# Gate folded into the attention values and the FFN, down and output projections in one bank, and an early third integer buffer, in a fused attention and gated-FFN kernel

## Chip, cores, metric

One core of one Trainium2 chip. The metric is the device time of the whole program in microseconds (us), as the median of several executions.

The engines by their short names: PE (TensorE, matrix products), ACT (ScalarE, activation functions), DVE (VectorE, elementwise), POOL (GpSimd), SP (the engine that here only issues DMAs).

## The reference

```python
g = sigmoid((x * gate_w).sum(-1, keepdims=True))          # x: 1 x 2048 x 512, bf16
q, k, v = split_heads(x @ wqkv)                           # 32 heads of width 16
p = softmax(q @ k.T * 16**-0.5);  a = (p @ v) @ wo
b = ((x @ w_gate) * (x @ w_up)) @ w_down                  # 512 -> 1376 -> 512
out = g * a + (1 - g) * b
```

Inputs are bf16. The exponentials dominate: 32 heads x 2048 x 2048.

## The kernel before

A small planner inside the kernel's Python code simulates the engines with fixed durations and fixes one static order of instructions for each engine. On the chip every engine works through its list in order and waits on semaphores. Whatever stands first in a list blocks all that is behind it.

The exponentials are done in *units* of 128 keys x 512 queries for one head; four units (four heads) of one key range are a *key tile*. There are 2048 units. ACT computes most with its Exp, two or three per instruction. DVE computes the others with integer arithmetic: four clamps from PSUM into an int16 buffer, and four shifted tables from that buffer, whose weighted values PE adds up. So a DVE tile takes four value passes of PE where an ACT tile takes one.

```python
D_START = 45.0                    # no DVE tile earlier on the planner's clock
D_SLOT = 0.3                      # how late DVE may be before a span takes a DVE unit as its third
FFN_FROM, FFN_TO = 60.0, 490.0    # FFN products due evenly over these key tiles
...
nb = (dst["buf"] + 1) % (3 if "k" in last_v else 2)     # third int16 buffer (wk) only after the last K product
...
# up: psX -> usb (copy);  gate: psX * usb -> hT;  down: psX * omg[:, t] -> bsb;  output: psX * gval[:, t] + bsb -> ost
...
def norm(m, last):                # after the last value pass of head group m
    for j in range(4):            # SP: numerators into place, then the denominators
        a = P.dma("sp", onum[r0 : r0 + 16, :] <- oraw[r0 : r0 + 16, s, :], dur=0.3)
    a = P.dma("sp", den[...] <- oraw[dr : 96 + dr + 1 : 32, s, :])
...                               # cut and abridged
def finish(...):                  # DVE: rec = 1 / den;  SP: rec -> DRAM -> rb, broadcast;  POOL: OT = onum * rb
...
fl.append((20, mk_gate(20)))      # gate unit due at key tile 20; Q of the second head block is due at 18
```

The softmax here doesn't subtract the row's maximum and nothing guards it: scores larger than these inputs give would overflow.

## Time and profile before

Three runs: 760.57 us median (760.49 to 761.5).

| | value | view |
|---|---|---|
| ACT busy | 735.3 us, 97% | first page |
| PE / DVE busy | 706.6 us (93%) / 677.7 us (89%) | first page |
| clamp copies, i.e. units on DVE | 440 of 2048 | groups |
| ACT in 168 to 740 us | busy 571.0 of 572 us | windows |

From the first page: the span, the busy time of each engine (us, share, instructions), and the chain of work that ended last.

```profile
span 759.2 us, 20945 instructions
...
PE 706.6 (93%) x8946; PEld 213.3 (28%) x8946; DVE 677.7 (89%) x1116; ACT 735.3 (97%) x672; POOL 65.2 (9%) x73
...
ACT 31%; DVE 30%; PE 30%; issue 6%; SPq 1%; DMA 1%; DVEq 0%; ACTq 0%
...
```

All three compute engines are close to full, and the chain passes through each of them for about 30%. From the groups by form (line, engine, operation, output<-input, shapes, count | busy us, mean ns of one | idle before it):

```profile
...
L1477 ACT ACTIVATE PT<-psS 128x1536 bf16<-128x1536 f32 x275 | 399.2, 1534 | 3.1 <-PE psS L889 2.8
L1477 ACT ACTIVATE PT<-psS 128x1024 bf16<-128x1024 f32 x386 | 386.9, 1111 | 5.6 <-PE psS L889 4.4 <-PE psX L985 0.7 <-PE psO L1120 0.2
...
L1042 DVE TENSOR_SCALAR SC<-SC 128x2048 int16<-128x2048 int16 x316 | 213.1, 692 | 2.2
L1013 DVE TENSOR_SCALAR SC<-psS 128x512 int16<-128x512 f32 x256 | 172.1, 682 | 15.1 <-PE psS L889 13.0 <-PE psX L985 1.6
...
L632 DVE CAST usb<-psX 128x512 bf16<-128x512 f32 x40 | 27.2, 680 | 0.8 <-PE psX L370 0.8
...
L683 DVE TENSOR_SCALAR bsb<-psX,omg 128x512 bf16<-128x512 f32 x16 | 11.6, 725 | 0.0
...
L708 DVE SCALAR_TENSOR_TENSOR ost<-psX,gval,bsb 128x512 bf16<-128x512 f32 x12 | 8.9, 743 | 2.5 <-PE psX L370 2.5
...
```

The table (L1042) and the clamp (L1013) take 0.69 and 0.68 us each on DVE; the up eviction (L632) 0.680, the scaled down eviction (L683) 0.725 and the combine (L708) 0.743. L1477 is the exponential in its three-unit and two-unit form. An ACT instruction overlaps the next by about 0.1 us. Measured from start to start where nothing waits, a two-unit exponential takes 0.904 us and a three-unit one 1.331 us. With these, the exponentials of this kernel are 720 us of pure ACT work. What the span has beyond that, from the first exponential on, is called *excess*: 29 us here, most of it before 140 us and in the last 10 us.

The windows early and in the main part (length, then busy time and instruction count of each engine, granted PE clock, DMA share and rate):

```profile
...
45.00:168.00 123.00, 112.11 (x1286) 31.95 (x1282) 102.63 (x167) 116.41 (x104) 5.44 (x4) 0.89 0.06 15
168.00:740.00 572.00, 538.10 (x6833) 159.95 (x6829) 548.30 (x901) 571.02 (x525) 17.08 (x13) 1.00 0.08 20
...
```

```profile
...
L509 SPq DMA_DIRECT2D QX<-Qst x8: 581/589/644, 44.0 to 48.5; - x8
...
DMA to landing us min/median/max: 1.8/1.8/3.0
```

DVE has 20 us to spare before 168 us and 24 us after.

### The profile page before, as it was taken

The numbers are of one execution on the slowest core, as the hardware profiler recorded it, in microseconds if no ns is written. First come the engines' busy times: TensorE is split into PE (matmuls) and PEld (weight loads), VectorE is DVE, ScalarE is ACT, GpSimd is POOL, SyncE is SP. The second block draws the span as 40 slices with busy tenths as digits, with TensorE's granted clock in tenths as the row PEclk, the third lists the DMA queues.
The fourth block names the chain that finished last, engine by engine and source line by source line (L and its number), as shares of the span: only waits on it lengthen the run. The fifth ranks groups of instructions, "written<-read, shape, count | busy, mean of one in ns | idle before, by whom it ended". The sixth has DMA issues, their size and how long they took to land.

```text
span 759.2 us, 20945 instructions
## 1 busy us (share of the span) xinstructions
PE 706.6 (93%) x8946; PEld 213.3 (28%) x8946; DVE 677.7 (89%) x1116; ACT 735.3 (97%) x672; POOL 65.2 (9%) x73
## 2 busy tenths in 40 slices
PE   9998898999899999998999999998999989899997
PEld 3322222222222322222222222222222222222243
DVE  3449987989999999999989989999999989999994
ACT  6989999999999999999999999999999999999995
POOL 8940000000000000000000000000000000000000
PEclk9978898999999999999999999999999999999999
DMA  8900000000010010101001010000001100010000
GB/s 173 284 16 9 16 15 25 16 9 24 9 30 9 23 38 11 29 9 28 12 10 31 29 30 10 24 15 9 24 10 28 40 19 16 7 29 8 24 23 31
DMA packets 32881, 22.81 MB, mean 30 GB/s; under 512 B 20468, under 2 KB 27572, under 8 KB 32788
## 3 DMA queue, kind: packets, MB, share of 16 engines
q1 hardware_dynamic: 31476, 20.42, 10.3%
q8 instruction: 71, 1.16, 0.7%
q0 software_dynamic: 256, 0.79, 0.4%
q10 hardware_dynamic: 1056, 0.26, 0.2%
q14 instruction: 22, 0.18, 0.1%
HBM read 11.24 MB, written 2.35 MB: 18 GB/s over the span
## 4 chain that ended last, share of the span: by engine, by line
ACT 31%; DVE 30%; PE 30%; issue 6%; SPq 1%; DMA 1%; DVEq 0%; ACTq 0%
ACT PT L1477 31%; DVE SC L1042 10%; PE psS L889 9%; DVE SC L1013 9%; PE psX L370 9%; PE psO L1120 8%; DVE wk L1013 4%; PE psS L370 1%; DVE hT L645 1%; DVE usb L632 1%; SPq L1180 1%; DVE wk L1042 1%; DMA den<-oraw 1%; DVE oraw L1173 1%; PE psO L1130 1%
## 5 line engine op out<-in xcount | busy, mean ns | idle before, releaser
L1477 ACT ACTIVATE PT<-psS 128x1024 bf16<-128x1024 f32 (+1 forms) x662 | 727.5, 1286 | 8.7 <-PE psS L889 7.2
L889 PE MATMUL psS<-QX,KT 32*128 32x512 bf16 x1966 | 265.0, 390 | 32.8 <-ACT PT L1477 21.3
L1042 DVE TENSOR_SCALAR SC<-SC 128x2048 int16<-128x2048 int16 x316 | 213.1, 692 | 2.2
L1013 DVE TENSOR_SCALAR SC<-psS 128x512 int16<-128x512 f32 x256 | 172.1, 682 | 15.1 <-PE psS L889 13.0
L1120 PE MATMUL psO<-PT,VV 128*32 128x512 bf16 x1546 | 150.1, 391 | 1.2 <-DVE oraw L1173 0.6
L889 PEld LDWEIGHTS psS<-QX,KT 32*128 32x128 bf16 x1966 | 68.6, 91 | 290.4 <-ACT PT L1477 113.9
L1120 PE MATMUL psO<-SC,VD 128*32 128x512 bf16 x1140 | 106.7, 389 | 4.1 <-DVE SC L1042 3.6
L1233 POOL TENSOR_TENSOR OT<-onum,rb 128x512 bf16<-128x512 f32 x16 | 21.3, 1332 | 674.0 <-DMA rb<-rscr 674.0
L1013 DVE TENSOR_SCALAR wk<-psS 128x512 int16<-128x512 f32 x102 | 68.5, 680 | 1.0 <-PE psS L889 0.7
L1042 DVE TENSOR_SCALAR SC<-wk 128x2048 int16<-128x2048 int16 x93 | 62.1, 688 | 0.1
L1120 PEld LDWEIGHTS psO<-PT,VV 128*32 128x32 bf16 x1546 | 38.6, 95 | 59.0 <-issue 48.2
L370 PE MATMUL psX<-xT,wu 128*32 128x512 bf16 x688 | 53.1, 394 | 1.0 <-DVE SC L1013 0.4
L370 PE MATMUL psX<-wd,hT 128*32 128x512 bf16 (+1 forms) x704 | 52.8, 382 | 0.1
L370 PE MATMUL psX<-xT,wg 128*32 128x512 bf16 x688 | 51.1, 383 | 0.6 <-DVE usb L632 0.2
L1120 PE MATMUL psO<-SC,VV 128*32 128x512 bf16 x428 | 43.3, 395 | 2.6 <-DVE oraw L1173 1.4
L1013 DVE TENSOR_SCALAR SC<-psX 128x512 int16<-128x512 f32 x60 | 40.7, 679 | 2.6 <-PE psX L985 2.6
L1120 PEld LDWEIGHTS psO<-SC,VD 128*32 128x32 bf16 x1140 | 28.1, 95 | 46.7 <-DVE SC L1042 27.2
L645 DVE TENSOR_TENSOR hT<-psX,usb 128x512 bf16<-128x512 f32 (+1 forms) x44 | 29.9, 680 | 3.6 <-PE psX L370 3.5
L985 PE MATMUL psX<-QX,KT 32*128 32x512 bf16 x82 | 32.2, 392 | 0.6 <-DVE hT L645 0.2
L632 DVE CAST usb<-psX 128x512 bf16<-128x512 f32 (+1 forms) x44 | 29.9, 680 | 0.8 <-PE psX L370 0.8
L1042 DVE TENSOR_SCALAR wk<-wk 128x2048 int16<-128x2048 int16 x31 | 21.8, 704 | 0.7
L1173 DVE COPY oraw<-psO 128x512 f32<-128x512 f32 x31 | 21.1, 681 | 0.5 <-PE psO L1120 0.5
(115 smaller groups left out, 363.9 us busy)
## 6 DMA issues: line engine op xcount, KB each, us to landing
rb<-rscr SPq DMA_DIRECT2D x16, 256.0 KB
onum<-oraw SPq DMA_DIRECT2D x124, 32.0 KB, 2.0
QX<-Qst SPq DMA_DIRECT2D x120, 16.0 KB, 1.8
out_dram<-ost SPq DMA_DIRECT2D x12, 128.0 KB, 1.8
wu<-in_B_w_up_dram SPq DMA_DIRECT2D x1, 1376.0 KB, 7.0
wg<-in_B_w_gate_dram SPq DMA_DIRECT2D x1, 1376.0 KB, 9.8
wd<-in_B_w_down_dram SPq DMA_DIRECT2D x1, 1280.0 KB, 12.7
SC<-in_A_x_dram SPq DMA_DIRECT2D x4, 128.0 KB, 3.2
```

The source lines that it names most:

```text
L370: r = pe.matmul(dst_[j : j + 32, :], lhs[:, j : j + 32], rhs, start=s0, stop=s1, tile_position=(0, j), skip_group_check=True,)
L632: "dve", lambda v: v.tensor_copy(usb[0:w, n % 2, :], un.bank[0:w, :]), deps, **EV
L645: lambda v: v.tensor_tensor(hT[0:w, f, :], un.bank[0:w, :], usb[0:w, n % 2, :], ALU.mult),
L889: q = pe.matmul(bank_ap(sl, k_), KT[32 * j : 32 * j + 32, b, kt * 128 : (kt + 1) * 128], QX[32 * j : 32 * j + 32, p, b, :], start=True, st ...
L985: lambda pe: pe.matmul(bank, KT[32 * j : 32 * j + 32, b, kt * 128 : (kt + 1) * 128], QX[32 * j : 32 * j + 32, p, b, :], start=True, stop=True,
L1013: lambda v: v.tensor_scalar(i2b(nb)[:, j, :], bank, _LO, _HI, ALU.max, ALU.min),
L1042: lambda v: v.tensor_scalar(dstt, src, 0.5, _BASE + _OFF[k], ALU.mult, ALU.add),
L1120: r = pe.matmul(psO[r_, :], vcol(m, kt, k_, j), pj, start=first, stop=last, tile_position=(0, 32 * j), skip_group_check=True)
L1130: r = pe.matmul(psO[r_, 256 * hf : 256 * hf + 256] if w < 2 else psD[r_, 0:256], vcol(m, kt, k_, j, hf) if w < 2 else ones[:, k_, 16 - 16 ...
L1173: o_ev[m] = P.op("dve", lambda v: v.tensor_copy(oraw[:, s, :], psO[:]), deps, **EV)
L1233: lambda g: g.tensor_tensor(OT[:, c % 2, b, :], onum[:], rb[:], ALU.mult),
L1477: lambda a: a.activation(cell_ap(cells[0], n).rearrange("p a b -> p (a b)"), bank_ap(sl, 0, n), ACT.Exp, scale=_LN2 / _OCT,),
```

## The change

Four intents. (1) Multiply the attention's normalisation by g and the up product by 1 - g, so that down and output projections accumulate in one PSUM bank with a single eviction. (2) Let `bsb` serve as a third integer buffer until `wk` is free, and start DVE tiles earlier. (3) Looser rules for giving DVE a unit. (4) A new timetable for the FFN products, Q projections six tiles earlier, the gate at tile 16 instead of 20, and value passes under more pressure. The core of the diff, cut:

```diff
-    D_START = 45.0
+    D_START = 38.0
-    D_SLOT = 0.3
+    D_SLOT = 0.6
-    FFN_FROM, FFN_TO = 60.0, 490.0
+    FFN = [(64, 160, 164, 5), (184, 270, 275, 5), (295, 385, 395, 4), (412, 478, 480, 5)]
+    gsc = nc.dram_tensor("gscr", [2, S], F32, kind="Internal").ap()
...
+                        for i, src_ in enumerate([gval, omg]):
+                            o = P.dma("pool", lambda e, i=i, src_=src_: e.dma_start(
+                                    gsc[i].rearrange("(t p) -> p t", p=128), src_[:], allow_slow_non_contiguous=True),
+                                [ogate["g"]], "dgs", dur=1.0, lat=20.0)
+                        ...   # 8 loads gscr -> gC (g beside the denominators), 1 load gscr -> omgB (1 - g, broadcast; 3 more follow later)
...
-                            "dve", lambda v: v.tensor_copy(usb[0:w, n % 2, :], un.bank[0:w, :]), deps, **EV
+                            lambda v: v.tensor_tensor(usb[0:w, n % 2, :], un.bank[0:w, :], omgB[0:w, :], ALU.mult),
...
+            return Unit(due, chain(FT + NB, mm), deps, drain)          # down and output in one bank, then one copy
...
-            nb = (dst["buf"] + 1) % (3 if "k" in last_v else 2)
+            nb = (dst["buf"] + 1) % 3
+                third[g, kt] = wk_i if "k" in last_v else bsb_i
...
+                r = P.op("dve", lambda v: v.tensor_tensor(rec[:, s, 0:w_], rec[:, s, 0:w_], gC[:, c, 0:w_], ALU.mult), ...)
...
-        fl.append((20, mk_gate(20)))
+        fl.append((16, mk_gate(16)))
-                n0 = 128 * c + 32 * b - 24
+                n0 = 128 * c + 32 * b - 30
...
+            press = sum(q_[1] is None for q_ in p_ring)
-            if pvs and not hold and (not fs or len(tails) or nr >= RP or len(pvs) - nr >= DP):
+            if pvs and not hold and (not fs or len(tails) or press >= RP or len(pvs) - nr >= DP):
```

More of the change, by code (lines that the diff above doesn't have):

```diff
@@ L168, in _build @@
     RU = 24
-    D_START = 45.0
+    D_START = 38.0
+    X_FILL = 45.0
     D_LEFT = 4
@@ L218, in _build @@
         usb = sb("usb", [128, 2, 512], BF16)
-        bsb = sb("bsb", [128, 5, D], BF16)
+        bsb = sb("bsb", [128, 4, D], BF16)
+        omgB = sb("omgB", [128, 512], F32)
+        gC = sb("gC", [128, NCH, 32], F32)
         ost = sb("ost", [128, 2, D], BF16)
@@ L566, in make @@
                             [un.free, o_vd, o_one],
-                            dur=0.75,
+                            dur=1.3,
                         )
@@ L575, in mk_v, with ld_omg @@
             return Unit(due, chain(KD, mm), lambda: [d_wv, ev_x[t]], drain)
-        ogate = {}
+        ogate, o_omg, gate_wait = {}, {}, []
+        def ld_omg(c, deps, eng="sp"):
+            o_omg[c] = P.dma(
+                eng,
+                lambda e: e.dma_start(omgB[:], bass.AP(gsc.tensor, gsc.offset + S + 512 * c, [[0, 128], [1, 512]])),
+                deps,
+                f"domg{c > 0}",
+            )
         def mk_gate(due):
@@ L608, in make @@
                         )
+                        for i, src_ in enumerate([gval, omg]):
+                            o = P.dma(
+                                "pool",
+                                lambda e, i=i, src_=src_: e.dma_start(
+                                    gsc[i].rearrange("(t p) -> p t", p=128), src_[:], allow_slow_non_contiguous=True
+                                ),
+                                [ogate["g"]],
+                                "dgs",
+                                dur=1.0,
+                                lat=20.0,
+                            )
+                        for i in range(8):
+                            p, j = i % 2, i // 2
+                            o1 = P.dma(
+                                "pool",
+                                lambda e, p=p, j=j: e.dma_start(
+                                    gC[32 * j : 32 * j + 32, :, 16 * p : 16 * p + 16],
+                                    bass.AP(gsc.tensor, gsc.offset, [[16, 32], [512, NCH], [1, 16]]),
+                                ),
+                                [o],
+                                "dgc",
+                                dur=1.0,
+                            )
+                        ogate["c"] = o1
+                        for dl in gate_wait:
+                            dl[-1] = o1
+                        ld_omg(0, [o], "pool")
                     dve_push(3, [e1], make)
@@ L627, in drain @@
                 if which == "u":
-                    deps = [last, u_free.get(n - 2)]
+                    deps = [last, u_free.get(n - 2), o_omg[c]]
                     def make():
                         ev_u[n] = un.free = P.op(
-                            "dve", lambda v: v.tensor_copy(usb[0:w, n % 2, :], un.bank[0:w, :]), deps, **EV
-                        )
+                            "dve",
+                            lambda v: v.tensor_tensor(usb[0:w, n % 2, :], un.bank[0:w, :], omgB[0:w, :], ALU.mult),
+                            deps,
+                            **EV,
+                        )
+                        if f == FT - 1 and c < NCH - 1:
+                            ld_omg(c + 1, [un.free])
                     dve_push(2, deps, make)
@@ L654, in deps @@
                 if which == "u":
+                    r.append(o_omg[c])
                     if n >= 2:
@@ L676, in drain @@
                     h_use[c] = last
-                deps = [last, ogate["g"], b_use.get(t - 5)]
+                deps = [last, last_v.get("b")]
                 def make():
-                    ev_b[t] = un.free = P.op(
-                        "dve",
-                        lambda v: v.tensor_scalar(bsb[:, t % 5, :], un.bank, omg[:, t : t + 1], None, ALU.mult),
-                        deps,
-                        dur=0.65,
-                        lat=0.1,
-                    )
+                    ev_b[t] = un.free = P.op("dve", lambda v: v.tensor_copy(bsb[:, tt, :], un.bank), deps, **EV)
                 dve_push(2, deps, make)
@@ L692, in deps @@
                 r = [d_wd] + [ev_h[c, f] for f in range(FT)]
-                if t >= 5:
-                    r.append(b_use[t - 5])
                 return r
@@ L708, in make @@
                     lambda v: v.scalar_tensor_tensor(
-                        dst, bank, gval[:, t : t + 1], bsb[:, t % 5, :], ALU.mult, ALU.add
+                        dst, bank, gval[:, t : t + 1], bsb[:, t % 4, :], ALU.mult, ALU.add
                     ),
@@ L724, in combine, with mk_dw, mm @@
             dve_push(2, deps, make)
-        def mk_wo(c, tt, due):
+        def mk_dw(c, tt, due):
             t = 4 * c + tt
-            def mm(pe, bk, b, s0, s1):
+            def mm(pe, bk, i, s0, s1):
+                if i < FT:
+                    w = FW[i]
+                    return cmm(pe, bk, hT[0:w, i, tt * 128 : (tt + 1) * 128], wd[0:w, i, :], s0, s1)
+                b = i - FT
                 return cmm(pe, bk, OT[:, c % 2, b, tt * 128 : (tt + 1) * 128], wo[:, b, :], s0, s1)
@@ L733, in drain, with make @@
                 if tt == 3:
-                    ot_use[c] = last
-                combine(t, un.bank, last, un)
+                    ot_use[c] = h_use[c] = last
+                deps = [last, o_out.get(t - 2)]
+                def make():
+                    o_comb[t] = un.free = P.op("dve", lambda v: v.tensor_copy(ost[:, t % 2, :], un.bank), deps, **EV)
+                    o_out[t] = P.dma(
+                        "sp",
+                        lambda e: e.dma_start(out2[t * 128 : (t + 1) * 128, :], ost[:, t % 2, :]),
+                        [o_comb[t]],
+                        f"dout{t % 2}",
+                    )
+                dve_push(2, deps, make)
             def deps():
-                r = [d_wo, ev_b[t]] + [o_mult[c, b] for b in range(NB)]
+                r = [d_wd, d_wo] + [ev_h[c, f] for f in range(FT)] + [o_mult[c, b] for b in range(NB)]
                 if t >= 2:
@@ L741, in deps @@
                 return r
-            return Unit(due, chain(NB, mm), deps, drain)
+            return Unit(due, chain(FT + NB, mm), deps, drain)
         def grp(m):
@@ L753, in _build @@
         on_d = {}
-        st = dict(gA=0, actE=None, actJ=0, gD=0, pvg=0, prog=0, i2=0)
+        st = dict(gA=0, actE=None, actJ=[], gD=0, pvg=0, prog=0, i2=0)
         def kq_deps(m, kt):
@@ L758, in kq_deps, with act_units @@
             return [ev_k[b, kt // 4 - (b == kt == 0)], q_dma[b, c, p]]
-        def act_units(n):
+        def act_units(n, but=None):
+            order = lambda js: sorted(js, key=lambda j: (j == but, j))
             r = []
-            g, e, j = st["gA"], st["actE"], st["actJ"]
+            g, e, js = st["gA"], st["actE"], order(st["actJ"])
             lf = {g: list(left[g])}
@@ L770, in act_units @@
                         break
-                    e, j = (g, lf[g].pop(0)), 0
-                r.append((e, j))
-                j += 1
-                if j == 4:
+                    e, js = (g, lf[g].pop(0)), order(range(4))
+                r.append((e, js.pop(0)))
+                if not js:
                     e = None
@@ L779, in take @@
             for e, j in units:
-                if j == 0:
+                if e != st["actE"]:
                     left[e[0]].remove(e[1])
-                st["actE"], st["actJ"] = (e, j + 1) if j < 3 else (None, 0)
+                    st["actE"], st["actJ"] = e, [0, 1, 2, 3]
+                st["actJ"].remove(j)
+                if not st["actJ"]:
+                    st["actE"] = None
                 st["gA"] = e[0]
@@ L827, in cap @@
         def cap(sl, now):
-            if sl and not xs[1]["res"] and now > D_START:
+            if sl and not xs[1]["res"] and now > X_FILL:
                 x_get(now)
@@ L872, in do_s @@
             if len(un) == 3 and spans and not overdue() and backlog(now) < min(need_s() - now, 1.5) + D_SLOT:
-                busy = {j for _, j in un[:2]}
-                j = d_can(now, busy)
-                if j is not None and j not in busy:
-                    dj, un, dh = j, un[:2], Hold()
+                if dst["e"] is not None or d_claim(now):
+                    for j in dst["js"]:
+                        two = act_units(2, j)
+                        if j not in [j_ for _, j_ in two]:
+                            dj, un, dh = j, two, Hold()
+                            break
             n = len(un)
@@ L929, in _build, with i2b @@
         wk_i = wk[:, :, :].bitcast(I16)
-        def i2b(nb):
-            return I2[:, nb, :, :] if nb < 2 else wk_i
+        bsb_i = bsb[:, :, :].bitcast(I16)
+        third = {}
+        def i2b(e):
+            return I2[:, on_d[e], :, :] if on_d[e] < 2 else third[e]
         def d_can(now, js_busy):
@@ L968, in d_claim @@
             on_d[g, kt] = nb
+            if nb == 2:
+                third[g, kt] = wk_i if "k" in last_v else bsb_i
             dst["cnt"] = 0
@@ L1007, in d_unit @@
                 st["prog"] += 1
-            d4 = [o, d_free[nb] or (last_x[0] if nb < 2 else last_v["k"])]
+            d4 = [o, d_free[nb] or (last_x[0] if nb < 2 else None)]
+            if nb == 2 and third[e] is wk_i:
+                d4.append(last_v["k"])
             def make():
@@ L1012, in make @@
                     "dve",
-                    lambda v: v.tensor_scalar(i2b(nb)[:, j, :], bank, _LO, _HI, ALU.max, ALU.min),
+                    lambda v: v.tensor_scalar(i2b(e)[:, j, :], bank, _LO, _HI, ALU.max, ALU.min),
                     d4,
@@ L1037, in make @@
                 def make():
-                    src = i2b(nb)[:, :, :].rearrange("p a b -> p (a b)")
+                    src = i2b(e)[:, :, :].rearrange("p a b -> p (a b)")
                     dstt = LL[:, k, :, :].rearrange("p a b -> p (a b)") if k < 3 else src
@@ L1042, in make @@
                         lambda v: v.tensor_scalar(dstt, src, 0.5, _BASE + _OFF[k], ALU.mult, ALU.add),
-                        pops + ([lf or last_x[0]] if k < 3 else done[:3]),
+                        pops + ([lf or last_x[0]] if k < 3 else []),
                         dur=0.6,
@@ L1084, in lview @@
             nb = on_d[e]
-            return (LL[:, k, j, :] if k < 3 else i2b(nb)[:, j, :]).bitcast(BF16)
+            return (LL[:, k, j, :] if k < 3 else i2b(e)[:, j, :]).bitcast(BF16)
         def vcol(m, kt, k, j, low=None):
@@ L1146, in do_pv @@
                     d_free[nb] = o
+                    if nb == 2 and third[e] is bsb_i:
+                        last_v["b"] = o
                     dst["p1"][nb] = None
@@ L1209, in make @@
                 r = P.op("dve", lambda v: v.reciprocal(rec[:, s, 0:w_], den[:, s, 0:w_]), dd + [norm_ops.get(("scr", blk - 2))], dur=0.25)
+                if c < NCH - 1:
+                    r = P.op(
+                        "dve",
+                        lambda v: v.tensor_tensor(rec[:, s, 0:w_], rec[:, s, 0:w_], gC[:, c, 0:w_], ALU.mult),
+                        [r, ogate["c"]],
+                    )
                 norm_ops["rec", blk] = r
@@ L1238, in make @@
                     assert c < 2 or (c - 2) in ot_use
-            dve_push(1, dd, make)
+            dl = dd + [ogate.get("c", "pending")]
+            if "c" not in ogate:
+                gate_wait.append(dl)
+            dve_push(1, dl, make)
         fl = []
@@ L1254, in _build @@
             for b in range(NB):
-                n0 = 128 * c + 32 * b - 24
+                n0 = 128 * c + 32 * b - 30
                 fl.append((n0, mk_q(b, c, n0)))
-        n_ffn = NCH * (2 * FT + 4)
-        a0, a1 = FFN_FROM, FFN_TO
-        q = 0
-        for c in range(NCH):
+        for c, (a0, a1, ad, dd) in enumerate(FFN):
             for f in range(FT):
-                for w in "ug":
-                    du = a0 + (a1 - a0) * q / n_ffn
+                for i, w in enumerate("ug"):
+                    du = a0 + (a1 - a0) * (2 * f + i) / (2 * FT)
                     fl.append((du, mk_ug(c, f, w, du)))
-                    q += 1
             for tt in range(4):
-                du = a0 + (a1 - a0) * q / n_ffn
-                fl.append((du, mk_d(c, tt, du)))
-                q += 1
-        for c in range(NCH - 1):
-            fl += [(128 * (c + 1) + 8 + 3 * tt, mk_wo(c, tt, 128 * (c + 1) + 8 + 3 * tt)) for tt in range(4)]
+                du = ad + dd * tt
+                fl.append((du, (mk_dw if c < NCH - 1 else mk_d)(c, tt, du)))
         fl.sort(key=lambda x: x[0])
@@ L1389, in step_pe @@
                 f = pick_fill(t + 0.3)
-                if t > D_START and any(isinstance(x["u"], Unit) for x in xs):
+                if t > X_FILL and any(isinstance(x["u"], Unit) for x in xs):
                     f = None
@@ L1417, in step_pe @@
             if pick == "pv":
-                it = next((q_ for q_ in pvs if (q_[1] is not None) == (nr < RP)), pvs[0])
+                it = next((q_ for q_ in pvs if (q_[1] is not None) == (press < RP)), pvs[0])
                 p_ring.remove(it)
```

## The prediction

> **What bounds the kernel now.** 2048 exponential units (128x512) are shared by two engines. ScalarE (ACT) is the limit: busy 735.3 of 759.2 us (first page), and by windows 571.0 of the 572 us between 168 and 740. Its 24 us of idle time lie in the prologue, in 45 to 140 us (about 6.6) and in the tail (9.7). So time moves by (1) units taken from ACT and (2) those early stalls. By groups ACT takes 1.45 us for three units and 1.00 for two: 0.45 us a unit plus 0.10 an instruction. VectorE (DVE) takes 440 units (the clamp copies), 110 key tiles; each tile needs 4 clamps of 0.68 us and 4 tables of 0.69, 5.45 us for four units that cost ACT 1.8. DVE is busy 677.7 us (89%), PE 706.6 (93%); a DVE tile needs four value passes where an ACT tile needs one, about 0.65 us more PE.
>
> **What the change does.**
> - Down and output projections of chunks 0 to 2 share a bank: twelve scaled evictions (0.73 us) vanish, twelve combines (0.74) become copies (0.68): -9.5 us DVE. PE products stay the same in number.
> - The up eviction becomes a product with an fp32 SBUF operand. The Trainium skill, "VectorE: DVE Perf Modes", section "Why PSUM operands drop a tier", caps fp32 with a PSUM operand at 1x; here the cast and the gate product from PSUM both take 0.680 us, so I expect no change.
> - Twelve gate products on denominators: about 0.18 us each (the 128x16 op took 0.174): +2. Net DVE -7 us.
> - The gate's round trip through DRAM: a few DMAs once, near 45 us. The first normalisation runs at 78 us, so at most a few us of DVE waiting.
> - A third integer buffer from the start instead of at 168 us (first clamp into wk), and DVE tiles from 38 instead of 45 us of the order's own clock. DVE is busy 8.2 of 15 us in 45 to 60, 94.5 of 108 in 60 to 168. I expect about 10 us of DVE idle recovered.
> - The looser slot rule (0.3 to 0.6) and free choice of the quarter let some more DVE units into the main part, where DVE is busy 548 of 572 us: perhaps 5 us.
>
> **Sum.** 7 + 10 + 5 = 22 us of DVE time, 4 more tiles, 16 units: ACT falls by 16 x 0.45 = 7.2 us; more two-unit instructions give back up to 1. Early ACT stalls shrink by 1 to 4. PE gains 2.6 us of work, which it can hold. The changed order of value passes I count as zero.
>
> Predicted: 751 us (-1.3%), 8 in 10 between 743 and 757. Faster by over 2%: 0.18; within 2%: 0.79; slower by over 2%: 0.03.
>
> **What will show it.** Clamp copies 452 to 464 instead of 440; ACT busy 726 to 730 us, still about 97%; DVE about 690 us, 92%; PE 709; up eviction still 0.68 us; bsb evictions four instead of sixteen; clamps into bsb before 168 us; DVE busy in 45 to 168 us up by about 10; ACT idle in 45 to 140 us below 6.
>
> **What would make it wrong.** The fp32 operand makes the up eviction slower (at 0.8 us, +5 us DVE). The gate's DMAs land late, and DVE, in order, stands behind the first normalisation while PE and ACT run dry. The longer hold of the spare bank (15 products in place of 11 or 4) or a crowded middle starves PE. The granted PE clock, 0.66 in 45 to 60 us, falls further or recovers entirely. The order may take many more DVE tiles than I allow: ten more would give 742.

## More of the kernel before

The Q loads of the second head block are issued from 44.0 to 48.5 us and land in 2 us.

## The result

779.23 us median (777.76 to 781.05, four runs) against 761.04 us (760.49 to 762.01, four runs): slower, ratio 1.0239 with a 95% interval of 1.0214 to 1.0264. A ratio here is always the mean time of one kernel's fast runs over that of the other's fast runs of the same rounds, so it is not quite the ratio of the medians quoted.

The first page of the changed kernel (777.4 us):

```profile
span 777.4 us, 21121 instructions
...
PE 715.6 (92%) x8982; PEld 212.3 (27%) x8982; DVE 697.9 (90%) x1164; ACT 729.7 (94%) x680; POOL 75.1 (10%) x84
...
DVE 41%; PE 34%; ACT 12%; DMA 4%; SPq 3%; issue 3%; POOL 1%; DVEq 0%; ACTq 0%
...
```

```profile
...
L1551 ACT ACTIVATE PT<-psS 128x1024 bf16<-128x1024 f32 x434 | 423.2, 1074 | 24.4 <-PE psS L950 22.2 <-PE psX L1052 0.9
L1551 ACT ACTIVATE PT<-psS 128x1536 bf16<-128x1536 f32 x235 | 335.4, 1500 | 7.8 <-PE psS L950 4.3 <-remote 3.1
...
L1111 DVE TENSOR_SCALAR SC<-SC 128x2048 int16<-128x2048 int16 x308 | 206.3, 709 | 4.4 <-remote 2.4 <-PE psO L1189 1.7
L1082 DVE TENSOR_SCALAR SC<-psS 128x512 int16<-128x512 f32 x273 | 183.0, 687 | 17.4 <-PE psS L950 16.7 <-PE psS L1052 0.5
...
L674 DVE TENSOR_TENSOR usb<-psX,omgB 128x512 bf16<-128x512 f32 x40 | 27.5, 687 | 0.2 <-PE psX L374 0.2
...
L782 DVE CAST ost<-psX 128x512 bf16<-128x512 f32 x12 | 8.2, 685 | 0.0
...
L728 DVE CAST bsb<-psX 128x512 bf16<-128x512 f32 x4 | 2.7, 684 | 0.9 <-PE psX L374 0.9
...
L1284 DVE TENSOR_TENSOR rec<-rec,gC 128x32 f32<-128x32 f32 x12 | 2.3, 192 | 0.4
...
```

The work has moved as intended. The sixteen bsb evictions are down to four (L728), the twelve combines became copies (L782), and all the clamp groups together are 464, so DVE has 116 tiles instead of 110. ACT is busy 729.7 instead of 735.3 us, and its pure work fell by 9.8 us, from 719.9 to 710.1. And yet the span is 18 us longer: ACT fell from 97% to 94% and from 31% to 12% of the chain. The excess grew from 29 to 57 us. The windows and the Q loads:

```profile
...
45.00:168.00 123.00, 102.42 (x1171) 28.24 (x1175) 106.66 (x178) 105.98 (x99) 14.86 (x16) 0.90 0.20 18
168.00:740.00 572.00, 537.77 (x6615) 153.50 (x6608) 551.38 (x917) 557.71 (x519) 19.12 (x13) 0.98 0.08 21
...
```

```profile
...
L513 SPq DMA_DIRECT2D QX<-Qst x8: 536/589/642, 53.8 to 58.2; - x8
...
DMA to landing us min/median/max: 13.0/13.6/13.8
```

ACT lost 10.4 us between 45 and 168 us (106.0 instead of 116.4) and 13.3 after it (557.7 instead of 571.0). And a Q load now takes 13 us to land where it took 2. The waits of the changed kernel (engine, line, what it waited for: us in total, times, longest):

```profile
...
ACT PT L1551 <- PE psS L950: 26.5, 26, 9.1
POOL gC L638 <- DMA gscr<-omg: 17.7, 1, 17.7
...
DVE rec L1280 <- DMA den<-oraw: 13.1, 11, 3.9
PE psS L950 <- DMA QX<-Qst: 12.3, 1, 12.3
...
ACT PT L1551 <- remote: 3.1, 1, 3.1
...
DVE SC L1111 <- remote: 2.4, 1, 2.4
...
```

The same view of the kernel before has no wait of PE for QX and none on "remote", and for the denominators and for ACT it has:

```profile
...
DVE rec L1209 <- DMA den<-oraw: 8.6, 9, 3.1
...
ACT PT L1477 <- PE psS L889: 7.2, 15, 0.9
...
```

A wait on "remote" is one for which the profile found no releaser; the section on b_hit and b_miss comes back to it.

So there are two suspects. The chain in order of time (start, length, what) shows the first:

```profile
...
53.44 0.61 DVE SC L1082
...
57.55 0.64 SPq L513
...
58.24 13.27 DMA QX<-Qst
...
71.64 0.61 PE psS L950 x3
...
```

PE needs the second head block's Q, and the last of its eight loads, issued at 58.2 us, lands at 71.5. About 4 us before the first of these loads, at 50.1 and 51.4 us, POOL had issued the two element-wise gate writes. They landed at 70.2 us, where POOL's wait of 17.7 us ends. Why they stand there can be read from the order of DVE's instructions. Before: Q eviction at 43.3 us, gate at 50.1 to 50.6. After: gate at 48.3 to 49.0, Q eviction at 49.8. The gate's due tile moved from 20 to 16, in front of Q's 18.

The second suspect shows in short windows around 590 us:

```profile
...
588.00:590.00 2.00, 1.50 (x18) 0.42 (x14) 1.13 (x2) 2.00 (x3) 0.00 (x0) 1.00 0.21 49
590.00:592.00 2.00, 0.00 (x0) 0.00 (x0) 0.56 (x3) 1.96 (x2) 0.00 (x0) 0.80 0.11 21
592.00:594.00 2.00, 1.36 (x11) 0.33 (x11) 2.00 (x4) 0.09 (x1) 0.00 (x0) 0.50 0.07 7
594.00:596.00 2.00, 2.00 (x16) 0.34 (x12) 1.68 (x3) 1.36 (x1) 0.00 (x0) 0.50 0.07 14
...
```

DVE stops, then PE stands still (no matmul from 589.8 to 592.6 us), then ACT; and from 591.2 us on PE's clock is granted at 0.50 for 6.8 us. DVE's wait is 2.3 us, ACT's excess around it 4.5 us. How much of the difference is the clock's was not tested apart. What DVE stood behind, and what SP was doing:

```profile
...
591.40 0.35 DVE L1280 RECIPROCAL rec<-den 128x32 f32<-128x32 f32 x1 [2.27 <-DMA den<-oraw]
...
```

```profile
...
581.97 4.95 SPq L513 DMA_DIRECT2D QX<-Qst  x8
586.97 2.50 SPq L1251 DMA_DIRECT2D onum<-oraw  x4
589.51 0.60 SPq L1261 DMA_DIRECT2D den<-oraw  x1
...
```

SP issues one DMA in about 0.6 us. The planner charged 0.3 to 0.5. Eight Q loads (now due six tiles earlier) and four numerator copies stood in front of the one denominator load that DVE's next instruction waits for. Of the sixteen denominator loads that DVE's reciprocals wait for, two have eight Q loads in the 9 us before them, those issued at 269.8 and 589.5 us, and DVE waits 1.95 and 2.27 us there. In the kernel before, none has.

### The profile page after: what moved, and what is told of

The parts are those of the page before. It is cut to its first block, busy times and chain, and to the rows that moved or that the text cites. A ratio compares the mean times of both kernels' runs of the same rounds, so it can differ in the third digit from the quotient of the medians.

```text
span 777.4 us, 21121 instructions
## 1 busy us (share of the span) xinstructions
PE 715.6 (92%) x8982; PEld 212.3 (27%) x8982; DVE 697.9 (90%) x1164; ACT 729.7 (94%) x680; POOL 75.1 (10%) x84
## 4 chain that ended last, share of the span: by engine, by line
DVE 41%; PE 34%; ACT 12%; DMA 4%; SPq 3%; issue 3%; POOL 1%; DVEq 0%; ACTq 0%
DVE SC L1111 15%; ACT PT L1551 12%; PE psS L950 11%; DVE SC L1082 11%; PE psX L374 10%; PE psO L1189 10%; DVE wk L1082 5%; SPq L1251 3%; DVE usb L674 2%; DMA den<-oraw 2%; DMA QX<-Qst 2%; DVE hT L691 2%; DVE oraw L1244 1%; DVE bsb L1082 1%; PE psS L374 1%
## 5 line engine op out<-in xcount | busy, mean ns | idle before, releaser
L950 PE MATMUL psS<-QX,KT 32*128 32x512 bf16 x1991 | 274.0, 391 | 39.1 <-ACT PT L1551 15.2
L1111 DVE TENSOR_SCALAR SC<-SC 128x2048 int16<-128x2048 int16 x308 | 206.3, 709 | 4.4 <-remote 2.4
L1082 DVE TENSOR_SCALAR SC<-psS 128x512 int16<-128x512 f32 x273 | 183.0, 687 | 17.4 <-PE psS L950 16.7
L1189 PE MATMUL psO<-SC,VD 128*32 128x512 bf16 x1208 | 115.0, 395 | 6.2 <-DVE SC L1111 5.3
L1082 DVE TENSOR_SCALAR wk<-psS 128x512 int16<-128x512 f32 x113 | 75.8, 687 | 6.0 <-PE psS L950 5.5
L374 PE MATMUL psX<-wd,hT 128*32 128x512 bf16 (+1 forms) x704 | 57.8, 392 | 2.4 <-DVE ost L782 1.9
L674 DVE TENSOR_TENSOR usb<-psX,omgB 128x512 bf16<-128x512 f32 (+1 forms) x44 | 30.2, 687 | 0.2 <-PE psX L374 0.2
L1082 DVE TENSOR_SCALAR SC<-psX 128x512 int16<-128x512 f32 x35 | 24.0, 687 | 0.8 <-PE psX L1052 0.6
L1052 PE MATMUL psX<-QX,KT 32*128 32x512 bf16 x55 | 21.6, 393 | 0.1
```

The costliest lines, as they stand in the source:

```text
L374: r = pe.matmul(dst_[j : j + 32, :], lhs[:, j : j + 32], rhs, start=s0, stop=s1, tile_position=(0, j), skip_group_check=True,)
L674: lambda v: v.tensor_tensor(usb[0:w, n % 2, :], un.bank[0:w, :], omgB[0:w, :], ALU.mult),
L950: q = pe.matmul(bank_ap(sl, k_), KT[32 * j : 32 * j + 32, b, kt * 128 : (kt + 1) * 128], QX[32 * j : 32 * j + 32, p, b, :], start=True, st ...
L1052: lambda pe: pe.matmul(bank, KT[32 * j : 32 * j + 32, b, kt * 128 : (kt + 1) * 128], QX[32 * j : 32 * j + 32, p, b, :], start=True, stop=True,
L1082: lambda v: v.tensor_scalar(i2b(e)[:, j, :], bank, _LO, _HI, ALU.max, ALU.min),
L1111: lambda v: v.tensor_scalar(dstt, src, 0.5, _BASE + _OFF[k], ALU.mult, ALU.add),
```

## The experiments

Each kernel ran three timed rounds, beside the kernel before on the same chip (760.4 to 762.1 us median in the four sessions). "Orders kept" means that the instruction order on PE, DVE, ACT and POOL was compared between the two kernels and is the same apart from the edit itself. Where a rule or duration of the planner is changed, the whole order is planned anew; the control b_spq below shows that this alone can move the time by 1%. The kernels were timed in four sessions on different chips, so kernels of different sessions are best compared by their ratios.

| kernel | median us | ratio to before (95%) |
|---|---|---|
| changed kernel | 779.23 | 1.0239 (1.0214 to 1.0264) |
| fx_gate | 764.71 | 1.0066 (1.0024 to 1.0109) |
| a_den | 769.81 | 1.0106 (1.0057 to 1.0155) |
| g_den (both faults mended) | 755.22 | 0.9922 (0.9885 to 0.9960) |
| gd_half | 763.33 | 1.0034 (1.0009 to 1.0059) |
| a_gate20 | 759.99 | 0.9993 (0.9964 to 1.0023) |
| gd_gate20 | 754.03 | 0.9909 (0.9872 to 0.9946) |
| b_hit / b_miss | 765.17 / 767.59 | 1.0063 (1.0019 to 1.0108) / 1.0083 (1.0044 to 1.0123) |
| b_den | 759.84 | 0.9993 (0.9968 to 1.0017) |
| b_spq | 767.92 | 1.0095 (1.0051 to 1.0139) |
| fx_both | 760.01 | 0.9990 (0.9943 to 1.0037) |
| fx_fill / fx_slot | 759.51 / 759.81 | 0.9974 (0.9935 to 1.0012) / 0.9980 (0.9943 to 1.0017) |
| gd_q24 / gd_press | 762.40 / 762.39 | 1.0014 (0.9987 to 1.0042) / 1.0034 (1.0002 to 1.0067) |
| gd_no3 | 759.77 | 0.9986 (0.9943 to 1.0029) |

All gave correct results.

### fx_gate: the gate written in rows

Gate and 1 - gate sit side by side in one 128x32 tile. One DVE transpose of 32x32 blocks turns it so that each partition holds 32 consecutive tokens of one row, and four DMAs write 32 rows of 128 bytes each. Orders kept: the new operations are entered into the planner at no cost.

```diff
-    gsc[i].rearrange("(t p) -> p t", p=128) <- src_[:]                    # i = 0, 1: 2048 elements each
+    v.transpose(gT[:], gv2[:])                                            # gv2 = [gval | omg]
+    bass.AP(gsc.tensor, gsc.offset + 32 * q, [[128, 32], [1, 32]]) <- gT[32 * q : 32 * q + 32, :]   # q = 0..3
```

> The changed kernel with the same instruction order on PE, ACT and SP; only the gate's two element-wise writes to DRAM (2 x 2048 elements of 4 bytes) become one 32x32-block transpose on DVE and four writes of 32 rows of 128 bytes. Theory 1 (the element-wise writes fill the DMA engines and hold back the QX loads that PE needs next): the QX landing falls from 13 us to about 2, PE's 12.3 us wait for QX is gone, time 779 -> 766 to 769. Rival (the order is packed too densely, with 116 DVE tiles and more two-unit exponentials, and the stall only surfaces there): it resurfaces elsewhere, time stays at 775 or above.

Measured: 764.71 us, 14.5 us less than the changed kernel, a little more than expected. The Q loads of this kernel:

```profile
...
L514 SPq DMA_DIRECT2D QX<-Qst x8: 534/589/590, 54.0 to 58.4; - x8
...
DMA to landing us min/median/max: 1.7/2.2/3.6
```

PE's wait for QX is 1.8 us instead of 12.3, and no wait on "remote" is left. POOL's wait for its gate write fell from 17.7 to 1.9 us. The first theory holds; the rival, that an order packed this densely would only stall elsewhere, falls. (The profiled run was the slowest of the four, 770.87 us; the other three lay within 764.5 to 764.9. Its trace is used for the waits and not for the total.)

### b_hit and b_miss: the same writes in the kernel before

```diff
+    for i in range(2):     # orders kept; dz is a zeroed 128x16 tile, gscr is read by nobody
+        P.dma("pool", gsc[i].rearrange("(t p) -> p t", p=128) <- dz[:], [dep])
     # b_hit: dep = eviction of the second block's Q      b_miss: dep = the gate
```

> The kernel before with every order kept, plus the same two element-wise writes (of a zeroed tile, read by nobody) issued by POOL when the first Q block is evicted, so that they run beside its QX loads (from 44 us). Theory 1: QX loads land late, PE waits for them, +6 to +12 us (767 to 773). Rival (element-wise writes are harmless; it was the order): within 1 us of before.

> The kernel before with every order kept, plus the same two element-wise writes issued when the gate is computed (50.6 us), when the QX loads have landed and the next loads needed are the denominators (78 us). Theory 1 (it is the coincidence, not the writes as such): within 2 us of before. If the writes cost time wherever they stand (POOL descriptor work, DMA share): +8 us or more here as well.

Measured: +3.1 and +5.5 us over the 762.08 us of before in the same session. Both expectations missed. In b_hit POOL was still busy and issued the writes at 48.8 us, when SP was at the last of the Q loads (45.0 to 49.5 us), so the coincidence that I wanted didn't come about. In b_miss the writes cost although PE never waits for Q loads and DVE's wait for denominators is as before (8.7 us). The waits show a second stall (b_hit, then b_miss):

```profile
...
ACT PT L1499 <- remote: 3.7, 1, 3.7
...
DVE SC L1035 <- remote: 3.6, 1, 3.6
...
```

```profile
...
ACT PT L1498 <- remote: 5.2, 1, 5.2
...
DVE KT L424 <- remote: 4.6, 1, 4.6
...
```

ACT and DVE stop together for 4 to 5 us. All five kernels with the full element-wise writes have such "remote" waits, of 2.4 to 5.2 us on ACT and DVE; gd_half (below), with half of them, has one of 1.7 us on ACT; before, fx_gate, g_den and gd_gate20 have none.

The packed trace shows who was late. These waits are for semaphores (counters that one engine raises and another waits for) that only PE's matmuls raise. In b_miss the matmul that frees ACT is recorded from 62.99 to 63.38 us, but its semaphore rises at 68.78. In each of the six kernels with element-wise writes the update that ends ACT's wait comes 2.1 to 5.4 us after the recorded end of its matmul. In the twelve kernels without them, none of the 138 to 166 such updates before 85 us comes over 0.3 us late. So PE was held up too, or at least its semaphores were. The changed kernel's 12.3 us therefore hold both stalls: PE's matmuls have no record from 59.4 to 71.6 us, but two of PE's semaphores rise at 61.7 and 61.8, so some 10 us are left for the Q loads.

What held PE is not shown. The page lists DMA queues of the kind "instruction", which bring the engines their instructions. In the changed kernel their packets at 57.4 and 60.8 us took 5.0 and 5.5 us, while the other instruction packets from 48 to 75 us took 0.3 to 1.2 us. The Trainium skill, "Runtime: NRT & Kernel Launch", section "Instruction fetch mechanics", says that each sequencer fetches its next block through a DMA queue of its own, mostly hidden. A late block was my first reading (the expectation for a_gate20 below still speaks of it), but the times don't bear it out: in b_miss the packet took a usual 1.2 us and came at 66.8 us, after the late matmuls had been recorded.

### fx_both: both faults mended in the planner

```diff
     QX <- Qst      -  dur=0.3            +  dur=0.6,  lat=1.6
     onum <- oraw   -  dur=0.3            +  dur=0.62, lat=1.6
     den, rscr      -  (dur=0.5, lat=2.2) +  dur=0.6,  lat=1.6
```

> fx_gate, and the order is planned with the issue times of SP that the trace shows (0.60 to 0.62 us for QX, onum, den, rscr in place of 0.3 to 0.5). Theory 2 (the rest of the loss is DVE standing behind a denominator that lands late because SP issues eight QX loads and four numerator copies before it, after which PE dries and its clock halves): excess of ACT at 260-280 and 580-600 us (3.8 and 4.5 us) goes, time 5 to 9 us below fx_gate, 758 to 763. Rival (the long hold of the bank by the merged projections is what stalls there): stalls in the projection phases stay, time within 2 us of fx_gate.

Measured: 760.01 us, 4.7 less than fx_gate. The time is within the span expected (the gain just short of 5 us), but the order is planned anew, and b_spq shows why this can't be read as a proof.

### b_spq: control

The same edit in the kernel before.

> Control for fx_both: the kernel before, its order planned with SP's measured issue times. DVE waited 8.6 us for denominators in before, most of it where nothing else suffers: within 2 us of before (758 to 763). If it gains 4 us or more, fx_both's gain over fx_gate was a fault of the old planner too and not of the change.

Measured: 767.92 us, +0.95%, with the same 110 tiles. Expected was no change. Correct durations in the planner made the old order worse; planning anew moved the time by 1% by itself. From here on the second theory was tested with orders kept.

### g_den: denominators first

```diff
 # fx_gate, in norm(); the planner is given the completion times it had before
-    4 x (onum <- oraw);  den <- oraw
+    den <- oraw;  4 x (onum <- oraw)
```

> fx_gate with PE, DVE, ACT and POOL in exactly the same order; only SP issues the denominator before the four numerator copies of the same group instead of after them, so that it lands about 2.4 us earlier. Theory 2 (DVE stands behind a late denominator at 260-280 and 580-600 us, PE dries, its clock halves): those two stalls (2.3 and 4.2 us of ACT excess in fx_gate) shrink to under 1 us each, time 4 to 6 us below fx_gate, about 760. Rival (the stalls come from holes in the projection schedule): within 2 us of fx_gate.

Measured: 755.22 us, 9.5 less than fx_gate (ratio to before 0.9922 instead of 1.0066): more than the 4 to 6 expected. (The two ran in different sessions; by the ratios the gain is 1.44%, about 11 us.) DVE's wait for denominators in this kernel:

```profile
...
DVE rec L1290 <- DMA den<-oraw: 1.9, 2, 1.3
...
```

It was 13.1 us in the changed kernel and 13.5 in fx_gate. Of the two stalls that were to shrink under 1 us, the first did (ACT excess 0.45 us), the second fell from 4.2 to 2.3. Half clock fell as well: leaving out the last stretch, PE ran 23.8 us at 0.5, against 47.7 in the changed kernel, 44.4 in fx_gate (in its slowest run) and 30.6 before. My reading of why 11.6 us less waiting by an engine that has slack is worth 9.5 us of span is the chain seen at 590 us: DVE holds up PE, PE's activity sinks, and the clock follows. The Trainium skill, "TensorE: Matmul & The Clock Gate", section "What's actually happening", describes a clock at half rate after an idle window of about 3.4 us. The half-clock stretches in these traces, but for the last, are 3.4, 6.8, 10.2 or 13.7 us long, which agrees. That PE must have been idle for a whole window does not: in the 3.4 us before the fall at 591.2 us PE was busy for 1.7 us, and before one at 83.3 us in the kernel before for 2.2 us.

### b_den and a_den: the other corners

The same exchange of DMAs in the kernel before, and in the changed kernel with its element-wise writes. Orders kept.

> Control for g_den: the kernel before, all orders kept, the denominator issued before the numerator copies. Before's DVE waited 8.6 us for denominators, but at most 3 us of that stood where ACT lost time. Theory 2 (the collision is made by the changed order, not by the old one): 0 to -3 us, 757 to 761, so that g_den stays the faster. Rival (den first is simply a gain of 9 us for any kernel): 751 to 753.

> The changed kernel with the denominators first and the element-wise gate writes kept: the fourth corner of the square of after (779), fx_gate (764.7), g_den (755.2). If the two losses are separate stalls at separate times, they add: 779 - 9.5 = about 769 to 771. If they are one loss seen twice (a late start of the planned order drifting through), 760 to 765 or 776 and above.

Measured: b_den 759.84 us (0.9993), no gain, although DVE's wait for denominators fell from 8.6 to 0.6 us. So the late denominators hurt the changed order and not the old one. a_den 769.81 us, as expected. The two losses are separate and add up: in ratio to before, the writes cost 1.73% with late denominators (1.0239 - 1.0066) and 1.84% with early ones (1.0106 - 0.9922); the late denominators cost 1.33% with element-wise writes and 1.44% with rows.

With orders kept, ACT's excess can be compared instruction by instruction. The changed kernel's and a_den's differ by 0.7 us up to 257 us and by 10.4 in the end; 7.0 of the difference arise at 257 to 280 and 564 to 590 us, the two places where Q loads stood ahead of a denominator. So the loss lies where theory 2 puts it.

### gd_half, a_gate20 and gd_gate20: amount and place of the writes

gd_half is g_den with only g written element by element, 2048 writes instead of 4096, orders kept. a_gate20 and gd_gate20 are a_den and g_den with the gate due at tile 20, so that it comes after the Q eviction; they differ from each other only in the writes. With the gate at tile 20 the order is planned anew (117 DVE tiles instead of 116).

> g_den with one of the two gate rows written element by element (2048 writes of 4 bytes in place of 4096), at the same place, right before the Q loads, all orders the same. g_den is 755, a_den 770. If the element count sets how long the DMA engines are held: about half of the 15 us, 761 to 765. If any element-wise write holds them as long: 768 to 771. If it is harmless below some amount: 755 to 757.

> a_den with the gate due at tile 20 as in before instead of 16, so that DVE makes the gate after the Q block (the changed kernel makes it just before) and the element-wise writes start when the Q loads are already issued. Coincidence: PE's wait for QX is below 2 us, what is left is the late instruction fetches, 3 to 5 us over gd_gate20, and 5 us or more below a_den, 758 to 764. If the writes cost 14 us wherever they stand: 12 us or more over gd_gate20.

> g_den with the gate due at tile 20: the partner of a_gate20, same order on PE, ACT and SP, gate written in rows. 117 DVE tiles and 708.3 us of pure ACT work against 116 and 710.1: 752 to 757.

Measured: gd_half 763.33, a_gate20 759.99, gd_gate20 754.03 us, each within its span of times (but a_gate20 is 6.0 us over gd_gate20 where I expected 3 to 5). In gd_half (two waits of its list):

```profile
...
POOL gC L653 <- DMA gscr<-gT: 10.0, 1, 10.0
...
PE psS L965 <- DMA QX<-Qst: 5.7, 1, 5.7
...
```

PE's wait for QX is 5.7 us, about half of a_den's 11.2, and POOL's for the write 10.0 instead of 16.9. With the gate after the Q loads, PE waits 0.3 us for QX and the writes cost 6.0 us (759.99 - 754.03), with "remote" waits of 4.0 us on ACT and 4.9 on DVE. So of the roughly 14 us, 3 to 6 come from the writes wherever they stand (3.1 in b_hit, 5.5 in b_miss, 6.0 here), and the rest from standing right before the Q loads.

### fx_fill, fx_slot, gd_q24, gd_press, gd_no3: single rules

fx_fill closes the gaps in the FFN timetable; fx_slot and gd_press set the slot rule and the pressure rule back; gd_q24 sets the Q lead back to 24; gd_no3 sets the early third buffer and the early start back. All are planned anew.

```diff
 fx_fill   (fx_both)  FFN = [(64, 164, 164, 5), (180, 275, 275, 5), (291, 395, 395, 4), (408, 480, 480, 5)]
 fx_slot   (fx_both)  D_SLOT = 0.3
 gd_press  (g_den)    press = nr
 gd_q24    (g_den)    n0 = 128 * c + 32 * b - 24
 gd_no3    (g_den)    D_START = 45.0;  nb = (dst["buf"] + 1) % (3 if "k" in last_v else 2)
```

> fx_both with the holes of the new FFN table closed (up and gate products of a chunk run to the start of its down products: 160->164, 270->275, 385->395, 478->480, starts 4 earlier). Theory 3 (between the last up/gate product and the first down product PE has no filling work, its clock is halved at 245 and 406 us, and work behind it stalls): halved clock after 100 us falls from 14 us to under 7, ACT excess from 37 to 33 us or less, time 3 to 5 us below fx_both, about 756. Rival (these clock drops come from the denser main loop itself): within 2 us of fx_both.

> fx_both with the slot rule back at 0.3 (113 DVE tiles in place of 115, ACT's pure work 714.9 in place of 711.6 us at 0.904 and 1.331 us an instruction). If the looser rule buys time, 2 to 4 us slower than fx_both; if its denser packing is what costs the excess (37 us against 29 in before), equal or up to 4 us faster.

> g_den with the Q projections due 24 instead of 30 tiles ahead, as in before (117 DVE tiles). If the earlier Q loads still collide with the normalisation on SP, 2 to 4 us faster than g_den (751 to 753); if den first has taken all of that, within 2 us of it.

> g_den with the old rule for value passes (only those ready count). I had counted that part as zero: within 2 us of g_den. ACT has more three-unit and fewer two-unit exponentials here (667 instructions in place of 673, pure work 709.7 in place of 710.1 us), so no gain from that; if the new rule is what keeps PE's banks free, 3 us or more slower.

> g_den without the early third buffer and with DVE tiles from 45 us again (115 tiles, pure ACT work 711.6 in place of 710.1). I credited this part with 10 us of DVE time, about 2 tiles and 3.5 us: 757 to 760. If the DVE idle time it fills is worth nothing because ACT and PE stall there anyway, 754 to 756.

Measured: fx_fill 759.51 and fx_slot 759.81 us, both within 1 us of fx_both. In fx_fill the half clock did not fall (34.1 us in both), so my third theory, gaps in the FFN timetable, has nothing for it. gd_q24 and gd_press came out 7 us slower than g_den, against both my expectations. gd_no3 came out 4.6 us slower, where I expected 2 to 5. But replanning alone moved b_spq by 7 us, and gd_q24 and gd_press were timed in another session than g_den, so none of these five settles what its rule is worth.

## Why the prediction was wrong

I predicted 751 us and got 779. Point by point:

- **DVE tiles and ACT work: right.** 464 clamps (I said 452 to 464), ACT busy 729.7 us (726 to 730), four bsb evictions, 28 clamps into bsb, the last at 167.3 us. DVE's and PE's busy times came a little above what I said (697.9 us for about 690, 715.6 for 709). The up eviction with the fp32 operand takes 0.687 us and so does the gate product beside it (0.680 both in the kernel before), so the statement in "VectorE: DVE Perf Modes" that I leaned on agrees with the trace.
- **The step that failed first: "The gate's round trip through DRAM: a few DMAs once, near 45 us ... at most a few us of DVE waiting."** I looked for its cost at its reader, the first normalisation. My list of risks had late gate DMAs, but with DVE as the one that waits. The cost was on others: 4096 writes of 4 bytes were under way until 70.2 us (issued at 50.1 and 51.4), and beside them Q loads from another engine's queue took 13 us, for which PE stood about 10 us, and PE's semaphores came late. Measured: 14.5 us (fx_gate). The Trainium skill had the warning, in "DMA: Bandwidth & Descriptors", section "Rules for kernel authors": a DMA whose last dimension isn't contiguous becomes one descriptor per element. The same page, section "Queues, rings and completion order", says that all queues share the same DMA engines, which take turns among them at packet granularity. I read past it because the transfer is only 16 KB.
- **The second, missing step: the SP queue.** The diff moves the Q loads by six tiles and I gave that line no term at all. With 0.6 us an issue, eight loads pushed two of the denominators back by about 5 us, and DVE stood behind them. That the six-tile shift brought them there is read from the traces and not tested with orders kept. Measured: 9.5 us (g_den against fx_gate), and no gain from the same exchange in the old order (b_den).
- **"Early ACT stalls shrink by 1 to 4": wrong in the changed kernel, right without the two collisions.** ACT lost 10.4 us more between 45 and 168 us. In g_den, DVE is busy 120.3 us in that window instead of 102.6 and ACT 119.4 instead of 116.4.
- **The sum comes into its range once both are taken away, in part by luck.** g_den measures 755.2 and gd_gate20 754.0 us. I had 751, with 743 to 757 as the range: a gain of 1.3%, and 0.8 to 0.9% came. In g_den pure ACT work fell by 9.8 us, more than the 6 to 7 forecast, and the early stalls shrank as forecast. But ACT also lost 5.9 us between 168 and 740 us (565.1 busy instead of 571.0), where I had counted no loss; the excess grew from 29 to 34 us. So the mechanism of the gain was right; one term came out larger than forecast, and a loss in the main part that I hadn't forecast took some of it back. The windows of g_den:

```profile
...
45.00:168.00 123.00, 114.32 (x1357) 31.96 (x1355) 120.32 (x203) 119.44 (x112) 15.56 (x19) 0.94 0.08 20
168.00:740.00 572.00, 541.30 (x6829) 157.66 (x6826) 550.19 (x915) 565.13 (x529) 18.91 (x14) 0.99 0.08 21
...
```

What stays open: which of the planner's rules earn the remaining 0.8 to 0.9%, since undoing a rule reorders everything; where the 5.9 us in the main part of g_den come from; what held PE in the second stall; and how 4-byte writes hold other DMAs back for so long. In the changed kernel the trace's DMA share is 0.30 from 64 to 66 us and under 0.02 from there to 70, while landings were still outstanding, so it isn't simply busy DMA engines.

gd_gate20 is faster than both kernels: 754.03 us, 0.9% below before (interval 0.5 to 1.3%). Its edits to the changed kernel are the gate in rows, the denominators first, and the gate due at tile 20.

## What to carry to other kernels

Cost a small DMA by its descriptors, and look for its price at everything that runs beside it and not only at its reader; a layout change on chip (here one transpose of 32x32 blocks, 0.21 us on DVE) was far cheaper than element-wise writes. Where the profile names no releaser, look up which engine raises that semaphore. When an edit moves loads, count the issues ahead of the load that an in-order engine waits for, and put the small one that gates others first. And test a planned kernel with its order held fixed: a replanned order differed by 1% by itself here.

## What the Trainium skill lacked or had wrong

- "DMA: Bandwidth & Descriptors" says that strided last dimensions lower to one descriptor per element but gives no time for such a DMA. Here 2 x 2048 element-wise 4-byte writes from SBUF to DRAM took about 19 us from the last issue to landing, and other queues' loads of 16 KB took 13 us beside them instead of 1.8, although the engines take turns among queues.
- The same page gives a fixed cost for a DMA but no measured time per issue on SP for a run of small ones on this chip: about 0.6 us each here, 2.5 us for four, which set the time at which a dependent engine could go on.
- No page says that such writes can hold up the matrix engine. In all six kernels that have them PE's semaphores rose 2.1 to 5.4 us after the recorded end of the matmul, and ACT and DVE stood for it; in the twelve without them none came over 0.3 us late at that time. The cause is open.
- "TensorE: Matmul & The Clock Gate" has the half clock right in steps of 3.4 us. It lets the clock fall after an idle window of about 3.4 us; here it fell after windows of that length in which PE was busy for 1.7 us (591.2 us in the changed kernel) and 2.2 us (83.3 us in the kernel before).
